# The z-gradient sums go to GpSimd, two on-chip transposes go to the DMA queue, and the bank border of the square products moves: one change to a forward-and-backward kernel of a transformer block

## The chip, the cores and the metric

The kernel runs on one core of a Trainium2 chip. The metric is device time in microseconds of one launch; the runs shown for the kernel before are 823.6, 823.75 and 826.96 us, median 823.75 us. The engines are named as in the profile: PE is the matrix engine (PEld its weight loads), DVE the vector engine, ACT the scalar engine, POOL is GpSimd, and SP is the engine whose queue issues most of the DMAs.

## What is computed

The reference computes a block and its gradients. With S = 2048 rows, D = 640 columns, 32 heads of 20 columns and F = 1728:

```python
# layer A: linear attention, on n = layernorm(x)
q, k, v = split(n @ wqkv)
pq, pk = phi(q), phi(k)                 # phi(t) = t+1 where t>0, else exp(t); plus 1e-6
kv = einsum("bhsd,bhse->bhde", pk, v)   # one 20x20 block per head
z  = einsum("bhsd->bhd", pk)
o  = (pq @ kv) / (pq . z + 1e-6)
h  = x + o @ wo
# layer B: gated MLP, on layernorm(h)
h2 = h + (silu(n2 @ w1) * (n2 @ w3)) @ w2
# results: h2 and the gradients of x, wqkv, wo, w1, w3, w2 for a given grad_out
```

Two intermediate gradients matter here. The gradient of z is a vector of 640 numbers: for each head it is the negative sum over all 2048 rows of r times sn, where r is the query feature divided by its denominator (`r_sb`, 16 tiles of 128 rows) and sn is one number per row and head. The gradient of kv is a 640 x 640 matrix that is not zero only near the 32 diagonal blocks.

## The kernel before

The rows are worked in 16 tiles of 128, the columns in 5 blocks of 128 (DT = 5; `M_H` lists the heads that touch each block). Nothing is reordered by a scheduler: each engine executes its instructions in the order in which the Python code emits them, and waits by semaphores for what others have to deliver. SP's queue is in order too, so an issue that waits holds up every later issue of that queue.

The stages that the change touches, in the order of time:

- **w2 gradient** (loop at line 1018). PE forms 13 products; meanwhile SP loads the transposed weights (`load_w13`, line 988) and the first two blocks of gated gradients (`load_gg`). The last 128 columns of the first weight set are turned on PE: `w13_tail` (line 992) makes 5 transposes, and a DVE copy puts them in place.
- **Stage b** (loop at line 1182, 16 rounds). In round t, PE forms the gradient at the layernorm output for tile t (`b_ghn`, 54 products in 6 parts), and between parts 4 and 5 the product `gr` of tile u = t - 2 (`b_gr`). DVE in each round: `g_h` of tile t - 1 (line 1095), `cc`, `pb` and the reduction `sn` of tile u (lines 1123, 1131, 1132), a negated copy of sn into 32 extra columns behind `g_h` (line 1133), then `wb` twice with two tiny operations between (lines 1085 to 1090), and the two operations of `b_gq` (lines 1138, 1139). POOL has one operation a round, `sz` (line 1135). ACT holds `gs` and `y` of the layernorm backward.
- **wo products** (`q_parts`, line 1143). PE multiplies `r_sb` with `g_h` in 20 parts of 8 products; the first parts stand between the last steps of stage b: part, transposes of `g_h` 14, 2 parts, `gr` 14, transposes of `g_h` 15, 2 parts, `gr` 15, and the rest. In half of them the moving side is 352 columns and not 320: the 32 extra columns carry the negated sn, so that the sums for the z gradient come out of the same products. Line 1160 masks them, line 1253 adds them up.
- **Squares** (`square`, line 1299). A 640 x 640 product with a block-diagonal side: for each of 5 blocks, 6 products, written into two PSUM banks. `SPLIT_D = 19` puts heads 0 to 18 in one bank and 19 to 31 in the other; the border falls inside block 2, so that block is cut into products of 140 and 20 columns. `unload` copies the banks out, one on ACT (380 columns) and one on DVE (260). There are 20 such squares: 5 in an early stage (`f2_wT`, line 686), 5 for `dwoT` (line 1327), 5 for `gm` (line 1352), and 5 in the loop at line 1369.
- **kv gradient**. `gkvT` is formed at line 1318. Its transpose `gkv_b` is made on PE, 13 transposes in the loop at line 1351, each group copied out by DVE. In the same loop the z gradient is spread over a diagonal (line 1360) and brought into all rows by 5 products with a matrix of ones (line 1364).
- **k gradient** (loop at line 1369). For each tile PE forms 10 products into one of 3 `dkv` buffers, DVE adds the z gradient (line 1378) and multiplies by the key features `pkb` (line 1379), which SP loads two tiles at a time (line 1344).

SP issues, around the squares: `xnT` 3, the transposing load of one third of wqkv (`load_wqT(0)`, line 1316), `mN` (line 1337), `dwoT` out (line 1338), four `pkb` loads, five transposes of `gm` (line 1361), `load_wqT(1)` in round 2 of the k loop (line 1393), and four transposing loads `pkT`.

Of the kernel before, what the change touches and what calls it, by code (L numbers as in the profile page):

```python
# [33 lines left out]

M_H = [_heads(m * P, (m + 1) * P, DH) for m in range(DT)]
M_MAX = max(b - a for a, b in M_H)
SPLIT_D = 19


def _pieces(ranges, split, width):  # L40
# [8 lines left out]


SQ = _pieces(M_H, SPLIT_D, DH)
SQ_BLOCKS = [(c, [m for m in range(DT) if M_H[m][0] * DH < (c + 1) * P and M_H[m][1] * DH > c * P]) for c in range(DT)]


@with_exitstack
def kernel(
# [51 lines left out]
    cp = pool("cp")  # L108
    U1 = pool("u1")
# [170 lines left out]
    def two(ap):  # L280
        return ap.rearrange("p (j n) -> p j n", j=2)
# [78 lines left out]
    def heads(ap):  # L360
        return ap.rearrange("p (h e) -> p h e", e=DH)
# [627 lines left out]
        dmaT(out=wT[0][:, 0:FT - 1, :], in_=B_w1[:, 0:F - FL])  # L989
        dmaT(out=wT[1][:], in_=B_w3[:, P - FL:F])  # L990

    def w13_tail():
        tr = ps.tile([P, DT, P], BF16, name="gw", bufs=4)
        for c in range(DT):
            T.transpose(tr[:, c, :], tail[:, c, :], ident[:])
        V.tensor_copy(out=wT[0][:, FT - 1, :].rearrange("p (c q) -> p c q", q=P), in_=tr[:])

    ggb = {}

# [18 lines left out]
    for fc in range(FT - 1):  # L1018
        b, i = divmod(fc, 4)
        if fc == FT - 2:  # L1020
            gw2_tail()
        acc = ps.tile([P, 2, 512], F32, name="gw", bufs=4)
        for j in range(2):
            for t in range(ST):
                T.matmul(acc[:, j, 0:HD], lhsT=hb[b][:, t, i * P:(i + 1) * P], rhs=g2[:, t, j * HD:(j + 1) * HD],  # L1025
                         start=(t == 0), stop=(t == ST - 1))
        ob = br.tile([P, D], BF16, name="gw2o", bufs=2)
        A.copy(out=ob[:].rearrange("p (j n) -> p j n", j=2), in_=acc[:, :, 0:HD])
        A.dma_start(out=out_6[fc * P:(fc + 1) * P, :], in_=ob[:])
# [8 lines left out]
        if fc == FT - 3:  # L1038
            w13_tail()
    ps.release()  # L1040
    U2.release()


    bl = pool("bl")
    g_hx = bl.tile([P, ST, D + H], BF16, name="g_h")
    g_h = g_hx[:, :, 0:D]
    g_q = bl.tile([P, ST, D], BF16, name="g_q")
    bo = pool("bo")
    r_sb = bo.tile([P, ST, D], BF16, name="r_sb")
    ps = pool("pbp", space=PSUM)  # L1050

    gz8 = cp.tile([P, DT, 8], F32, name="gz8")
    V.memset(gz8[:], 0.0)
    gz = cp.tile([P, DT], F32, name="gz")
    hnb, ghT, ln_rest = {}, {}, {}

    def b_load(t):
# [54 lines left out]
        ghT[t] = br.tile([P, DT, P], BF16, name="ghT", bufs=2)  # L1112
        A.copy(out=ghT[t][:], in_=tr[:])

    gr, cc, sz = {}, {}, {}

    def per_head(ap):
        return ap.unsqueeze(2).to_broadcast([P, H, DH])

    def b_gr(t):  # L1120

        cc[t] = br.tile([P, D], F32, name="cc")
        V.tensor_tensor(out=heads(cc[t][:]), in0=heads(r_sb[:, t, :]), in1=per_head(rden[:, t, :]), op=ALU.min)
        gr[t] = ps.tile([P, 2, 512], F32, name="gr", bufs=2)
        for j in range(2):
            for c in range(DT):
                T.matmul(gr[t][:, j, 0:HD], lhsT=ghT[t][:, c, :], rhs=wT2[:, c, j * HD:(j + 1) * HD], start=(c == 0),  # L1127
                         stop=(c == DT - 1))
        pb = br.tile([P, D], F32, name="pb")
        sn = br.tile([P, H], F32, name="sn", bufs=2)  # L1130
        V.tensor_tensor(out=two(pb[:]), in0=gr[t][:, :, 0:HD], in1=two(r_sb[:, t, :]), op=ALU.mult)
        V.reduce_sum(out=sn[:], in_=heads(pb[:]), axis=AX.X)
        V.tensor_scalar(out=g_hx[:, t, D:], in0=sn[:], scalar1=-1.0, scalar2=None, op0=ALU.mult)  # L1133
        sz[t] = br.tile([P, D], F32, name="sz")
        G.tensor_tensor(out=heads(sz[t][:]), in0=heads(Zb[:]), in1=per_head(g_hx[:, t, D:]), op=ALU.mult)  # L1135

    def b_gq(t):
        V.tensor_tensor(out=two(sz[t][:]), in0=gr.pop(t)[:, :, 0:HD], in1=two(sz[t][:]), op=ALU.add)
        V.tensor_tensor(out=g_q[:, t, :], in0=sz.pop(t)[:], in1=cc.pop(t)[:], op=ALU.mult)

    tri = {}

    def q_parts():

        acc = {}
        tags = ("ghn", "ghn", "gr", "ghn", "ghn")
        order = [(0, 0, 0), (0, 0, 1), (1, 0, 0), (1, 0, 1), (0, 8, 0), (1, 8, 0), (2, 0, 0), (2, 0, 1), (0, 8, 1),
                 (1, 8, 1), (2, 8, 0), (2, 8, 1)]
        order += [(m, t0, j) for m in (3, 4) for t0 in (0, 8) for j in range(2)]
        for m, t0, j in order:  # L1150
            if m not in acc:
                acc[m] = ps.tile([P, 2, 512], F32, name="gwo", tag=tags[m], bufs=2)
            n = HD + H * j
            for t in range(t0, t0 + 8):
                T.matmul(acc[m][:, j, 0:n], lhsT=r_sb[:, t, m * P:(m + 1) * P],  # L1155
                         rhs=g_hx[:, t, j * HD:j * HD + n], start=(t == 0), stop=(t == ST - 1))
            if (t0, j) == (8, 1):
                a, b = M_H[m]
                A.copy(out=two(qp[:, m, :]), in_=acc[m][:, :, 0:HD])
                V.tensor_tensor(out=gz8[:, m, 0:b - a], in0=acc.pop(m)[:, 1, HD + a:HD + b], in1=mask[:, m, 0:b - a, 0],  # L1160
                                op=ALU.mult)
                dmaT(out=QT[:, :, m * P:(m + 1) * P], in_=qp[:, m, :])
            yield

# [17 lines left out]
    for t in range(ST):  # L1182
        g = b_ghn(t)

        def part():
            next(g, None)

        u = t - 2
        ahead = 2 <= t <= ST - 4 and t % 2 == 0
        if ahead:  # L1190
            load_gg(t // 2 + 1, 0, FT)
        part()
        part()
        part()
        if t + 2 < ST:
            b_load(t + 2)
        if t >= 1:
            ln_rest.pop(t - 1)()
            if by_dma(t - 1):
                b_gT(t - 1)  # L1200
            if t <= 2 * DT:
                n = (t - 1) % DT
                dst, src = (woT, A_wo) if t <= DT else (kvN, kvT_d)
                A.dma_start_transpose(out=dst[:, :, n * P:(n + 1) * P], in_=src[n * P:(n + 1) * P, :])
            if ahead:
# [12 lines left out]

    tri = U1.tile([P, 2 * DT, D], BF16, name="tri", tag="S0")
    QT, qp = (tri[:, k * DT:(k + 1) * DT, :] for k in range(2))  # L1220
    qg = q_parts()

    def part(n=1):
# [10 lines left out]
    def load_wqT(k):  # L1234
        dmaT(out=wqT[:, k * DT:(k + 1) * DT, :], in_=A_wqkv[:, k * D:(k + 1) * D])
# [100 lines left out]
    gzd = small[:, 3 * DT, :].rearrange("p (m q) -> p m q", q=P)  # L1336
    dma(out=mN, in_=m_v)
    dma(out=rows(dwoT_d), in_=dwoT[:])

# [8 lines left out]
    for n in range(4):  # L1348
        load_pk(n)

    for i, (c, ms) in enumerate(SQ_BLOCKS):
        unload(square(wqT[:, 2 * DT:, :], gkvT, i), gm[:, i, :])
        tr = ps.tile([P, len(ms), P], BF16, name="trk", tag="dkv", bufs=3)
        for k, m in enumerate(ms):
            T.transpose(tr[:, k, :], gkvT[:, m, c * P:(c + 1) * P], ident[:])
        V.tensor_copy(out=gkv_b[:, c, ms[0] * P:(ms[-1] + 1) * P].rearrange("p (i q) -> p i q", q=P), in_=tr[:])
        fill(1)
        if i == 0:
            for m in range(DT):
                V.tensor_scalar(out=gzd[:, m, :], in0=ident[:], scalar1=gz[:, m:m + 1], scalar2=None, op0=ALU.mult)  # L1360
        dmaT(out=wqT[:, 2 * DT:, i * P:(i + 1) * P], in_=gm[:, i, :])
    acc = d_acc()
    for m in range(DT):
        T.matmul(acc[:, m // 4, m % 4 * P:(m % 4 + 1) * P], lhsT=ones[:], rhs=gzd[:, m, :], start=(m % 4 == 0),
                 stop=True, skip_group_check=True)
# [141 lines left out]
```

## Time and profile before

| what | value |
|---|---|
| median of three runs | 823.75 us (823.6 to 826.96) |
| span of the profiled execution | 821.9 us (first to last instruction) |
| median less span | 1.85 us, what lies around the instructions |
| PE busy | 814.4 us |
| PE, from 97 us to the end | busy 720.67 of 725 us |
| DVE, 402 to 538 us (stage b) | busy 90.96 of 136 us |
| POOL, 402 to 538 us | busy 16.65 of 136 us |
| granted clock of TensorE | 1.00 |

The span is that of one profiled execution, so a sum of its rows is compared with 821.9 us, and the 1.85 us are added for a time. "Busy" is the share of time in which an instruction of the engine runs; the chain of waits goes back from the last instruction, at each step to what released it or to the instruction before it.

### The profile page before, as it was taken

To read this page: it belongs to the slowest core of one execution; us is meant where nothing else is said; L and a number is where in the kernel's file an instruction comes from. 1 tells how busy PE (TensorE), PEld (TensorE's weight loads), DVE (VectorE), ACT (ScalarE), POOL (GpSimd) and SP (SyncE) were. 2 spreads that over 40 slices of the span, in tenths; PEclk is the share of its full clock that TensorE was granted. 3 is DMA by queue.
4 is the path that set the end of the run, shared out by engine and by line. 5 is a ranking of instruction groups with operands and counts; after the bars stand their busy time and mean duration, and the time that the engine had idled before them with its cause. 6 is when DMAs were issued, how large, how long until landed. Compare 5 with 4: busy or idle time off the path is not lost.

```text
span 821.9 us, 14179 instructions
## 1 busy us (share of the span) xinstructions
PE 814.4 (99%) x5522; PEld 522.6 (64%) x5549; DVE 453.1 (55%) x961; ACT 325.0 (40%) x609; POOL 133.1 (16%) x194
## 2 busy tenths in 40 slices
PE   8999999999999999999999999999999999999998
PEld 6677544555555555777777777767777777555554
DVE  7869887999898566300057777772681545200000
ACT  7856688665565666011122212222212334211111
POOL 2243333323223212100001111110220000000000
PEclk9999999999999999999999999999999999999999
DMA  9999889696485556999677897258984898885771
GB/s 233 254 279 227 207 234 312 196 242 157 145 213 155 166 181 162 250 241 267 195 170 179 206 204 188 70 113 178 268 216 93 164 200 181 201 199 137 165 170 38
DMA packets 320883, 157.26 MB, mean 191 GB/s; under 512 B 238704, under 2 KB 314064, under 8 KB 320816
## 3 DMA queue, kind: packets, MB, share of 16 engines
q1 hardware_dynamic: 278768, 115.54, 61.3%
q0 software_dynamic: 7328, 24.48, 8.9%
q10 hardware_dynamic: 34720, 16.34, 8.7%
q8 instruction: 43, 0.70, 0.4%
q14 instruction: 24, 0.20, 0.1%
HBM read 47.01 MB, written 51.13 MB: 119 GB/s over the span
## 4 chain that ended last, share of the span: by engine, by line
PE 94%; DVE 2%; ACT 1%; DMA 1%; issue 0%; SPq 0%; POOL 0%; DVEq 0%; ACTq 0%
PE mm L386 20%; PE job L1271 20%; PE ghn L1070 14%; PE gxn L1429 8%; PE o L833 7%; PE gw L1025 7%; PE gwo L1155 3%; PE big L266 3%; PE gr L1127 3%; PE dkv L1375 3%; PE macc L416 2%; PE at L642 2%; DMA wqkv<-in_A_wqkv_dram 1%; PE dkv L1303 1%; DVE st L147 1%; DMA Wp<-pkx 1%
## 5 line engine op out<-in xcount | busy, mean ns | idle before, releaser
L1271 PE MATMUL job<-gb,hnN 128*128 128x432 bf16 (+2 forms) x656 | 117.0, 342 | 0.0
L1070 PEld LDWEIGHTS <-ggb 128*128 128x128 bf16 x864 | 84.5, 98 | 32.8
L1271 PEld LDWEIGHTS <-hnN 128*128 128x128 bf16 x656 | 63.6, 98 | 53.4
L386 PE MATMUL mm<-pqT,w 128*128 128x512 bf16 x397 | 93.1, 379 | 0.5
L386 PEld LDWEIGHTS <-w 128*128 128x128 bf16 x540 | 52.5, 98 | 63.1 <-issue 0.8
L1275 ACT CAST obs<-job 128x432 bf16<-128x432 f32 (+3 forms) x61 | 29.3, 480 | 123.1 <-PE job L1271 123.1
L833 PE MATMUL o<-w,hhT 128*128 128x320 bf16 x448 | 67.7, 299 | 0.1
L1070 PE MATMUL ghn<-w13a,ggb 128*128 128x320 bf16 x448 | 63.5, 299 | 0.0
L1070 PE MATMUL ghn<-w13b,ggb 128*128 128x320 bf16 x416 | 61.4, 299 | 0.0
L386 PE MATMUL mm<-g2T,w2T 128*128 128x512 bf16 x227 | 58.5, 379 | 0.6
L833 PEld LDWEIGHTS <-hhT 128*128 128x128 bf16 x448 | 43.8, 98 | 23.8 <-issue 0.2
L1025 PE MATMUL gw<-g,hb 128*128 128x320 bf16 x416 | 56.8, 299 | 0.0
L1135 POOL TENSOR_TENSOR sz<-Zb,g_h 128x640 f32<-128x640 bf16 x16 | 20.2, 1260 | 198.8 <-DVE g_h L1133 107.7
L1025 PEld LDWEIGHTS <-hb 128*128 128x128 bf16 x416 | 40.6, 98 | 16.0 <-issue 0.3
L1429 PE MATMUL gxn<-wqT,gT 128*128 128x320 bf16 x320 | 48.7, 299 | 0.0
L406 ACT CAST ghh<-mm 128x512 bf16<-128x512 f32 x48 | 28.3, 590 | 44.7 <-PE mm L386 39.0
L772 ACT ACTIVATE sig<-mm 128x512 bf16<-128x512 f32 x56 | 33.9, 605 | 25.1 <-PE mm L386 21.6
L1082 ACT ACTIVATE gs<-ghn 128x640 bf16<-128x640 f32 x16 | 11.2, 703 | 78.9 <-PE ghn L1070 73.4
L386 PEld LDWEIGHTS <-w2T 128*128 128x128 bf16 x260 | 25.4, 98 | 23.3
L266 PEld LDWEIGHTS <-pqT 128*128 128x128 bf16 x320 | 30.6, 98 | 14.4 <-issue 1.7
L1429 PEld LDWEIGHTS <-gT 128*128 128x128 bf16 x320 | 31.3, 98 | 12.2
L266 PE MATMUL big<-wqkv,pqT 128*128 128x320 bf16 x250 | 38.5, 299 | 0.3
(210 smaller groups left out, 1282.3 us busy)
## 6 DMA issues: line engine op xcount, KB each, us to landing
hh_d<-hhT SPq DMA_DIRECT2D x24, 256.0 KB, 2.8
gg_d<-gate POOLq DMA_DIRECT2D x24, 256.0 KB, 4.1
gg_d<-ghh POOLq DMA_DIRECT2D x24, 256.0 KB, 3.5
ggb<-gg_d SPq DMA_DIRECT2D x6, 896.0 KB, 5.4
ggb<-gg_d ACTq DMA_DIRECT2D x6, 832.0 KB, 5.7
out_dram<-obs ACTq DMA_DIRECT2D x39, 108.0 KB, 3.0
x_sb<-in_A_x_dram SPq DMA_DIRECT2D x6, 640.0 KB, 5.4
ggb<-gg_d SPq DMA_DIRECT2D x2, 1728.0 KB, 13.5
```

Source lines behind the costliest of these rows:

```text
L266: T.matmul(acc, lhsT=pqT[:, c, t * P:(t + 1) * P], rhs=wqkv[:, c, n0:n0 + HD], start=(c == 0), stop=(c == DT - 1))
L386: T.matmul(acc[:], lhsT=w[:, c, fc * P:(fc + 1) * P], rhs=rhs[:, c, :], start=(c == 0), stop=(c == DT - 1))
L406: A.copy(out=ghh[n // 2][:, n % 2, :], in_=acc[:])
L772: A.activation(sig[:, i, :], gp[:], AF.Sigmoid)
L833: T.matmul(o2["ps"][:, 0:HD], lhsT=hhT[c][:, fc, i * P:(i + 1) * P], rhs=w2[:, fc, j * HD:(j + 1) * HD], start=(fc == 0), stop=(fc == FT - 1))
L1025: T.matmul(acc[:, j, 0:HD], lhsT=hb[b][:, t, i * P:(i + 1) * P], rhs=g2[:, t, j * HD:(j + 1) * HD], start=(t == 0), stop=(t == ST - 1))
L1070: T.matmul(acc[:, j, 0:HD], lhsT=ggb[t // 2][:, k, lo:lo + P], rhs=rhs[:, j * HD:(j + 1) * HD], start=(k == 0), stop=(k == NG - 1))
L1127: T.matmul(gr[t][:, j, 0:HD], lhsT=ghT[t][:, c, :], rhs=wT2[:, c, j * HD:(j + 1) * HD], start=(c == 0), stop=(c == DT - 1))
L1155: T.matmul(acc[m][:, j, 0:n], lhsT=r_sb[:, t, m * P:(m + 1) * P], rhs=g_hx[:, t, j * HD:j * HD + n], start=(t == 0), stop=(t == ST - 1))
L1271: T.matmul(acc[:, 0:n], lhsT=lhs[:, t, m * P:(m + 1) * P], rhs=rhs(t), start=(t == 0), stop=(t == ST - 1))
L1275: A.copy(out=ob, in_=acc[:, 0:n])
L1429: T.matmul(acc[:, j, 0:HD], lhsT=g, rhs=wqT[:, k, j * HD:(j + 1) * HD], start=(k == 0), stop=(k == 14))
```

## The change

- The 32 extra columns are gone, and with them line 1133, the mask step (line 1160), the sums (line 1253), the diagonal (line 1360). Instead POOL, after its `sz`, multiplies `r_sb` by sn for the tile and subtracts the product from a running sum `gza` (new `b_gz`); at the end DVE splits `gza` into two bfloat16 halves `gzs`, and four products of 320 columns with the ones matrix give the sum over rows.
- `rs`, POOL's product, takes the buffer of `pb`. `sz` is now subtracted and not added.
- The weight tail is turned by one DMA transpose at the end of `load_w13`; the 5 PE transposes and the copy go.
- The 13 PE transposes of `gkvT` and their copies go; five DMA transposes are issued on SP ahead of `mN`.
- `load_wqT(0)` moves from ahead of the kv gradient to round 2 of the k loop, `load_wqT(1)` from round 2 to round 4.
- `SPLIT_D` is 16: block 2 is cut into 80 and 80 columns, the copies are 320 and 320.

```diff
-SPLIT_D = 19
+SPLIT_D = 16
...
         dmaT(out=wT[0][:, 0:FT - 1, :], in_=B_w1[:, 0:F - FL])
         dmaT(out=wT[1][:], in_=B_w3[:, P - FL:F])
-    def w13_tail():
-        tr = ps.tile([P, DT, P], BF16, name="gw", bufs=4)
-        for c in range(DT):
-            T.transpose(tr[:, c, :], tail[:, c, :], ident[:])
-        V.tensor_copy(out=wT[0][:, FT - 1, :].rearrange("p (c q) -> p c q", q=P), in_=tr[:])
+        dmaT(out=wT[0][:, FT - 1, :].rearrange("p (c q) -> p c q", q=P), in_=tail[:].rearrange("p c f -> p (c f)"))
...
-    g_hx = bl.tile([P, ST, D + H], BF16, name="g_h")
-    g_h = g_hx[:, :, 0:D]
+    g_h = bl.tile([P, ST, D], BF16, name="g_h")
...
+    gza = br.tile([P, D], F32, name="gza")
+    G.memset(gza[:], 0.0)
...
         V.reduce_sum(out=sn[:], in_=heads(pb[:]), axis=AX.X)
-        V.tensor_scalar(out=g_hx[:, t, D:], in0=sn[:], scalar1=-1.0, scalar2=None, op0=ALU.mult)
         sz[t] = br.tile([P, D], F32, name="sz")
-        G.tensor_tensor(out=heads(sz[t][:]), in0=heads(Zb[:]), in1=per_head(g_hx[:, t, D:]), op=ALU.mult)
+        G.tensor_tensor(out=heads(sz[t][:]), in0=heads(Zb[:]), in1=per_head(sn[:]), op=ALU.mult)
...
+    def b_gz(t):
+        rs = br.tile([P, D], F32, name="rs", tag="pb")
+        G.tensor_tensor(out=heads(rs[:]), in0=heads(r_sb[:, t, :]), in1=per_head(sns.pop(t)[:]), op=ALU.mult)
+        G.tensor_tensor(out=gza[:], in0=gza[:], in1=rs[:], op=ALU.subtract)
...
-            n = HD + H * j
             for t in range(t0, t0 + 8):
-                T.matmul(acc[m][:, j, 0:n], lhsT=r_sb[:, t, m * P:(m + 1) * P],
-                         rhs=g_hx[:, t, j * HD:j * HD + n], start=(t == 0), stop=(t == ST - 1))
+                T.matmul(acc[m][:, j, 0:HD], lhsT=r_sb[:, t, m * P:(m + 1) * P],
+                         rhs=g_h[:, t, j * HD:(j + 1) * HD], start=(t == 0), stop=(t == ST - 1))
...
         if u >= 0:
             b_gq(u)
+            b_gz(u)
...
-    V.reduce_sum(out=gz[:], in_=gz8[:], axis=AX.X)
+    V.tensor_copy(out=gzs[:, 0, :], in_=gza[:])
+    V.tensor_tensor(out=gzs[:, 1, :], in0=gza[:], in1=gzs[:, 0, :], op=ALU.subtract)
...
     load_xnT(3)
-    load_wqT(0)
     fill(4)
...
+    for m in range(DT):
+        dmaT(out=gkv_b[:, :, m * P:(m + 1) * P], in_=gkvT[:, m, :])
     dma(out=mN, in_=m_v)
...
-        tr = ps.tile([P, len(ms), P], BF16, name="trk", tag="dkv", bufs=3)
-        for k, m in enumerate(ms):
-            T.transpose(tr[:, k, :], gkvT[:, m, c * P:(c + 1) * P], ident[:])
-        V.tensor_copy(out=gkv_b[:, c, ms[0] * P:(ms[-1] + 1) * P].rearrange("p (i q) -> p i q", q=P), in_=tr[:])
         fill(1)
...
-    for m in range(DT):
-        T.matmul(acc[:, m // 4, m % 4 * P:(m % 4 + 1) * P], lhsT=ones[:], rhs=gzd[:, m, :], start=(m % 4 == 0),
-                 stop=True, skip_group_check=True)
-    for x, y, bank in ((0, 4 * P, 0), (4 * P, D, 1)):
-        A.copy(out=gzb[:, x:y], in_=acc[:, bank, 0:y - x])
+    for j in range(2):
+        for k in range(2):
+            T.matmul(acc[:, j, 0:HD], lhsT=ones[:], rhs=gzs[:, k, j * HD:(j + 1) * HD], start=(k == 0), stop=(k == 1))
+    A.copy(out=two(gzb[:]), in_=acc[:, :, 0:HD])
...
-        if t == 2:
-            load_wqT(1)
+        if t in (2, 4):
+            load_wqT(t // 2 - 1)
```

More of the change, by code (lines that the diff above doesn't have):

```diff
@@ L51 @@
 SQ = _pieces(M_H, SPLIT_D, DH)
-SQ_BLOCKS = [(c, [m for m in range(DT) if M_H[m][0] * DH < (c + 1) * P and M_H[m][1] * DH > c * P]) for c in range(DT)]
 @with_exitstack
@@ L1037 @@
             load_gg(1, 0, NG)
-        if fc == FT - 3:
-            w13_tail()
     ps.release()
@@ L1050 @@
     ps = pool("pbp", space=PSUM)
-    gz8 = cp.tile([P, DT, 8], F32, name="gz8")
-    V.memset(gz8[:], 0.0)
-    gz = cp.tile([P, DT], F32, name="gz")
+    gza = br.tile([P, D], F32, name="gza")
+    G.memset(gza[:], 0.0)
     hnb, ghT, ln_rest = {}, {}, {}
@@ L1113, in b_gT @@
         A.copy(out=ghT[t][:], in_=tr[:])
-    gr, cc, sz = {}, {}, {}
+    gr, cc, sz, sns = {}, {}, {}, {}
     def per_head(ap):
@@ L1129, in b_gr @@
         pb = br.tile([P, D], F32, name="pb")
-        sn = br.tile([P, H], F32, name="sn", bufs=2)
+        sn = sns[t] = br.tile([P, H], F32, name="sn", bufs=2)
         V.tensor_tensor(out=two(pb[:]), in0=gr[t][:, :, 0:HD], in1=two(r_sb[:, t, :]), op=ALU.mult)
         V.reduce_sum(out=sn[:], in_=heads(pb[:]), axis=AX.X)
-        V.tensor_scalar(out=g_hx[:, t, D:], in0=sn[:], scalar1=-1.0, scalar2=None, op0=ALU.mult)
         sz[t] = br.tile([P, D], F32, name="sz")
-        G.tensor_tensor(out=heads(sz[t][:]), in0=heads(Zb[:]), in1=per_head(g_hx[:, t, D:]), op=ALU.mult)
+        G.tensor_tensor(out=heads(sz[t][:]), in0=heads(Zb[:]), in1=per_head(sn[:]), op=ALU.mult)
     def b_gq(t):
-        V.tensor_tensor(out=two(sz[t][:]), in0=gr.pop(t)[:, :, 0:HD], in1=two(sz[t][:]), op=ALU.add)
+        V.tensor_tensor(out=two(sz[t][:]), in0=gr.pop(t)[:, :, 0:HD], in1=two(sz[t][:]), op=ALU.subtract)
         V.tensor_tensor(out=g_q[:, t, :], in0=sz.pop(t)[:], in1=cc.pop(t)[:], op=ALU.mult)
+    def b_gz(t):
+        rs = br.tile([P, D], F32, name="rs", tag="pb")
+        G.tensor_tensor(out=heads(rs[:]), in0=heads(r_sb[:, t, :]), in1=per_head(sns.pop(t)[:]), op=ALU.mult)
+        G.tensor_tensor(out=gza[:], in0=gza[:], in1=rs[:], op=ALU.subtract)
     tri = {}
@@ L1152, in q_parts @@
                 acc[m] = ps.tile([P, 2, 512], F32, name="gwo", tag=tags[m], bufs=2)
-            n = HD + H * j
             for t in range(t0, t0 + 8):
-                T.matmul(acc[m][:, j, 0:n], lhsT=r_sb[:, t, m * P:(m + 1) * P],
-                         rhs=g_hx[:, t, j * HD:j * HD + n], start=(t == 0), stop=(t == ST - 1))
+                T.matmul(acc[m][:, j, 0:HD], lhsT=r_sb[:, t, m * P:(m + 1) * P],
+                         rhs=g_h[:, t, j * HD:(j + 1) * HD], start=(t == 0), stop=(t == ST - 1))
             if (t0, j) == (8, 1):
[L1158 to L1161, printed above, removed]
+                A.copy(out=two(qp[:, m, :]), in_=acc.pop(m)[:, :, 0:HD])
                 dmaT(out=QT[:, :, m * P:(m + 1) * P], in_=qp[:, m, :])
@@ L1213 @@
             b_gq(u)
+            b_gz(u)
         if t >= 4:
             load_xn(t - 4, t - 3)
-    tri = U1.tile([P, 2 * DT, D], BF16, name="tri", tag="S0")
-    QT, qp = (tri[:, k * DT:(k + 1) * DT, :] for k in range(2))
+    tri = U1.tile([P, 2 * DT + 2, D], BF16, name="tri", tag="S0")
+    QT, qp, gzs = tri[:, 0:DT, :], tri[:, DT:2 * DT, :], tri[:, 2 * DT:, :]
     qg = q_parts()
@@ L1244 @@
     b_gr(a)
+    b_gz(b)
     part()
     b_gq(a)
+    b_gz(a)
     part(3)
@@ L1335 @@
     mN, gkv_b, gm = (small[:, n:n + DT] for n in (0, DT, 2 * DT))
-    gzd = small[:, 3 * DT, :].rearrange("p (m q) -> p m q", q=P)
+    for m in range(DT):
+        dmaT(out=gkv_b[:, :, m * P:(m + 1) * P], in_=gkvT[:, m, :])
     dma(out=mN, in_=m_v)
@@ L1349 @@
         load_pk(n)
-    for i, (c, ms) in enumerate(SQ_BLOCKS):
+    for i in range(DT):
         unload(square(wqT[:, 2 * DT:, :], gkvT, i), gm[:, i, :])
-        tr = ps.tile([P, len(ms), P], BF16, name="trk", tag="dkv", bufs=3)
-        for k, m in enumerate(ms):
-            T.transpose(tr[:, k, :], gkvT[:, m, c * P:(c + 1) * P], ident[:])
-        V.tensor_copy(out=gkv_b[:, c, ms[0] * P:(ms[-1] + 1) * P].rearrange("p (i q) -> p i q", q=P), in_=tr[:])
         fill(1)
-        if i == 0:
-            for m in range(DT):
-                V.tensor_scalar(out=gzd[:, m, :], in0=ident[:], scalar1=gz[:, m:m + 1], scalar2=None, op0=ALU.mult)
         dmaT(out=wqT[:, 2 * DT:, i * P:(i + 1) * P], in_=gm[:, i, :])
     acc = d_acc()
-    for m in range(DT):
-        T.matmul(acc[:, m // 4, m % 4 * P:(m % 4 + 1) * P], lhsT=ones[:], rhs=gzd[:, m, :], start=(m % 4 == 0),
-                 stop=True, skip_group_check=True)
-    for x, y, bank in ((0, 4 * P, 0), (4 * P, D, 1)):
-        A.copy(out=gzb[:, x:y], in_=acc[:, bank, 0:y - x])
+    for j in range(2):
+        for k in range(2):
+            T.matmul(acc[:, j, 0:HD], lhsT=ones[:], rhs=gzs[:, k, j * HD:(j + 1) * HD], start=(k == 0), stop=(k == 1))
+    A.copy(out=two(gzb[:]), in_=acc[:, :, 0:HD])
     for t in range(ST):
```

## Prediction

> **What bounds the kernel now.** I read the page's busy times first, then the slices, then the chain of waits around the changed stages, then the timelines of DVE, POOL and SP there.
>
> ```profile
> span 821.9 us, 14179 instructions
> ...
> PE 814.4 (99%) x5522; PEld 522.6 (64%) x5549; DVE 453.1 (55%) x961; ACT 325.0 (40%) x609; POOL 133.1 (16%) x194
> ...
> PE   8999999999999999999999999999999999999998
> ...
> POOL 2243333323223212100001111110220000000000
> ```
>
> PE works without a gap: from 97 us to the end it is busy for 720.67 of 725 us, at a granted clock of 1.00, and what is missing there is the wait for the last DMA. Every stage that the change touches but the first squares lies behind 97 us, so a product taken from PE is worth its full spacing, and nothing taken from another engine is worth anything by itself. The reverse is the danger: a wait that the change brings to PE is paid in full, because nothing later can win it back. So there are two sums: what PE loses in work, and what it gains in waits.
>
> **The work taken from PE.** The chain of waits, from 535 to 630 us (start, length, who, how many), has each piece:
>
> ```profile
> 538.09 1.09 PE gwo L1155 x8
> ...
> 539.46 2.28 PE gwo L1155 x16
> ...
> 573.61 0.33 PE dkv L1303 x6
> ...
> 576.88 0.17 PE trk L1355 x3
> ...
> 582.84 0.28 PE dkv L1364 x5
> ```
>
> - Extra columns. Eight products of 320 columns take 1.09 us; the sixteen in the second line are eight of 320 and eight of 352, so eight wide ones take 2.28 - 1.09 = 1.19. There are ten wide groups: 10 x 0.10 = **-1.0 us** (-1.1 if every digit is kept).
> - Transposes of the kv gradient. Five groups, 0.11 + 3 x 0.17 + 0.11 = **-0.73 us**. Weight tail: five transposes, the same kind as in the last line, 0.28: **-0.28 us**.
> - z gradient by ones. Five products of 128 columns (0.28) become four of 320 at 0.136: 0.54, so **+0.26 us**.
> - Squares. The six products take 0.33; the 140-column ones in line 1322 take 1.56/25 = 0.062 each, so 0.02 is left for the 20-column one. From 140 to 320 columns a product grows by 0.074 in 180, so 80 columns take about 0.038, and two of them 0.076 against 0.082. I take -0.01 for a square, 15 squares behind 97 us: **-0.15 us**. Between nothing and -0.3. The five squares ahead of 97 us feed a chain of copies and transposes; ACT's copy gets 60 columns shorter and DVE's 60 longer, and I cost that at nothing, +-0.1.
>
> Together -1.9 us. The DVE operations that go (line 1133 at 0.18, the copies at 0.28 to 0.35, line 1360) are worth nothing: DVE is not on the chain there.
>
> **Wait one: POOL beside DVE in stage b.** A round is 8.69 us (7.33 of `ghn` and 1.36 of `gr` on the chain). One round of DVE and POOL in the timeline:
>
> ```profile
> 449.61 0.82 DVE L1132 TENSOR_REDUCE sn<-pb 128x32 f32<-128x640 f32 x1
> 450.47 0.18 DVE L1133 TENSOR_SCALAR g_h<-sn 128x32 bf16<-128x32 f32 x1
> 450.79 1.26 POOL L1135 TENSOR_TENSOR sz<-Zb,g_h 128x640 f32<-128x640 bf16 x1 [7.43 <-DVE g_h L1133]
> ...
> 452.02 0.83 DVE L1085 SCALAR_TENSOR_TENSOR wb<-gs,hnb 128x640 f32<-128x640 bf16 x1 [1.38 <-ACT gs L1082]
> ...
> 453.09 0.88 DVE L1090 SCALAR_TENSOR_TENSOR wb<-hnb,s,gs 128x640 f32<-128x640 bf16 x1
> ```
>
> `sz` runs while DVE waits for ACT, so the two never meet now. The change puts two more operations of 640 columns behind `sz`. The product `rs` has the shape of `sz`: 1.26. The subtraction reads two float32 operands, which no row shows on POOL; from below 1.26, from above 2.2, if the part of 1.26 that grows with the columns (0.95, from 0.79 at 320 columns to 1.26 at 640) doubled with the bytes. I take 1.26, the row with the same columns. So POOL is busy from 450.6 to 454.5, just where DVE has `wb`, `wb` again, `b_gq` and `g_h`. What meeting costs is seen in an earlier stage:
>
> ```profile
> 67.34 1.53 POOL L358 TENSOR_TENSOR pr<-pql,Zb 128x320 f32<-128x320 bf16 x2 [2.20 <-DVE rden L365]
> 67.69 0.48 DVE L368 TENSOR_SCALAR rden<-rden 128x32 f32<-128x32 f32 x1
> ...
> 68.59 0.97 DVE L372 TENSOR_TENSOR hx<-hx,rden 128x640 bf16<-128x640 bf16 x1
> ```
>
> Line 368 takes 0.18 where POOL is quiet, and line 372, which reads two operands from SBUF, 0.82; here 0.48 and 0.97. POOL's two end at 68.13 and 68.87; 68.17 - 0.18 = 67.99 and 69.56 - 0.82 = 68.74, so both run as if they had started 0.14 us ahead of such an end. The reduction of line 365, with one operand, is no slower under POOL (0.476 against 0.483). So a DVE operation with two SBUF operands waits out a POOL operation. In stage b these are `wb` twice, `g_q`, `g_h` and `cc`: 0.83 + 0.88 + 0.82 + 0.48 + 0.82 = 3.8 us a round, and POOL's three hold 3 x 1.12 = 3.4. That is 7.2 of 8.69, so they fit, but not without waits. Laid out: `wb` wants to start at 452.02, `rs` holds until 453.0; `wb` ends at 453.8 and lets `gza` in, which holds until 454.8; the second `wb` ends at 455.7, 1.7 late. The idle 0.7 ahead of `pb` takes some of it back; carried through the rounds the lag stays at 1.2 to 1.4 and is 1.8 at `g_h` 15. In the middle rounds nobody notices, since `gr` comes two rounds after its `g_h`. At the end PE does: its transposes of `g_h` 15 start at 543.10, and `g_h` 15 is ready at 542.9. Slack about nothing, cost **+1.8 us**. Bounds: 0, if the pieces happen to pass each other, and 15, in the rival below.
>
> [...]
>
> **Wait two: SP ahead of the k gradient.**
>
> ```profile
> 569.65 4.18 SPq L1235 DMA_TRANSPOSE wqT<-in_A_wqkv_dram  x1
> 573.97 0.50 SPq L1337 DMA_DIRECT2D small<-m_d  x1
> 574.94 0.38 SPq L1338 DMA_DIRECT2D dwoT_d<-dwoT  x1
> 575.50 3.88 SPq L1344 DMA_DIRECT2D pkb<-pk_d  x4
> ```
>
> The `mN` issue at 573.97 comes when PE has ended the last `dwoT` square (573.94 on the chain), since its buffer lies over what that square reads. The five new transposes go into the same buffer, so in the changed program the first of them carries this wait, and `mN`, `dwoT` out and `pkb` stand behind all five. The `load_wqT(0)` that is taken away lay ahead of the wait, under cover. Turning 128 x 640 out of SBUF costs SP 1.28 where the queue is quiet (`tri`, two in 2.55) and about 2.0 where it is full (`gm`, five in 9.93). The queue is emptier now, so five at 1.28: 6.4, to 580.4. `mN` then lands after 4.1 (800 KB row: 4.0; 5.9 now, behind the load that goes), 584.5; `dwoT` 2.6 behind it as now, 587.1; the first `pkb` 0.7 later, 587.8. Now it lands at 575.50 + 7.7 = 583.2. DVE wants it at 585.45 less the 0.5 that PE has gained by then. It waits, the three `dkv` buffers fill, and tile 3, due on PE at 588.45 - 0.5 = 587.9, gets its buffer after line 1379 and line 1378 (0.83 each) at 589.5: **+1.6 us**, once, since DVE then has all it needs. Bounds: 0 (lands in time) and 5.6 (transposes at 2.1).
>
> Costed at nothing: the weight tail's DMA shifts the first `ggb` (lands at 394.9, used at 401.7) by 1.3 to 2; the two `load_wqT` come some 10 us later but are first read by `gxn` at 628, and SP is free from 608.9 to 617.9. If that cover failed, `gxn` would start late by what is missing. POOL's sum for tile 15 ends near 560, its copy is needed at 582.
>
> **Sum.** 821.9 - 1.9 + 1.8 + 1.6 = 823.4; with the 1.85 between span and median, **825.2 us**, +0.2%. Half a per cent, 4.1 us, is about what a measurement of this kernel can tell from no change.
>
> **Rivals.**
> 1. *POOL sets the pace of stage b (slower).* DVE's own work is 6.7 us a round. If POOL's operations follow each other before a waiting DVE operation gets in, as at 60.67 us, where line 297 takes 1.86 instead of 0.32 across two of them, a round is 6.7 + 3.4 = 10.1, 1.4 too long, 14 times, less what falls into idle time: +5 to +15, 829 to 838. It decides from 2.0 us of waits a round (8.69 - 6.7). For it: the unknown third operation. Against: line 368 got in between two POOL operations each time, and `gza` waits for `rs`. Chance 0.2.
> 2. *The waits don't come (work only).* -1.9, with one of the two waits at most: 821.8 to 823.5. For it: POOL's turns may fall beside `pb`, `sn` and the `sz` sum, which have one SBUF operand at most. Chance 0.23.
> 3. *SP's transposes at full-queue price.* 825.2 + 4.0 = 829.2. For it: the `gm` rows, and a DMA share of 1.06 from 570 to 580. Chance 0.1.
> 4. My forecast, 823.5 to 828, has 0.47. That the change is not what it says is out: the built order of PE lacks 18 transposes and 80 wide products.
>
> Faster by over half a per cent (below 819.6) would need more than all of the removed work: 0.04. Slower (above 827.9) are rivals 1 and 3 and the edge of my own: 0.33. Within: 0.63. The range 821.2 to 833 leaves out 0.08 below and 0.1 above.
>
> **What would show it.** Line 1085's and 1090's rows of `wb` longer than 0.83 and 0.88, or starting behind POOL's end; a PE gap ahead of the transposes of `g_h` 15 (line 1111) that `g_h` ended; five DMA transposes at 1.3 each from PE's last `dwoT` square, `pkb` landing 12 us after that square, DVE idle ahead of the first `g_k`, and one PE gap of 1 to 2 us in the k loop. If stage b has the same length and no `wb` is late, wait one is wrong; if rounds are longer than 8.69, rival 1 holds.

## The result, and the profile after

The changed kernel takes **836.85 us** (median of five runs, 835.23 to 838.47), the kernel before 823.62 us beside it: ratio 1.0156, 95% interval 1.0142 to 1.017. The forecast was 825.2 us in a range of 821.2 to 833.0: the sign of the shift was right, the size was not, and the time lies outside the range. The profiled execution took 835.23 us, its span is 833.5 us, 11.6 more than before.

The page of the changed kernel, its first line, the line of busy times, and the slices of PE, POOL and the granted clock:

```profile
span 833.5 us, 14169 instructions
...
PE 817.2 (98%) x5503; PEld 522.8 (63%) x5530; DVE 473.2 (57%) x929; ACT 324.7 (39%) x608; POOL 190.6 (23%) x227
...
PE   8999999999999999999999999989799999999998
...
POOL 2243433332223212000035456551120000000000
PEclk9999999999999999999999999999899999999999
```

PE has two dents now, in slices 27 and 29 of 40, and the clock has one digit below full speed. The products are 19 fewer, and yet PE's busy time went up by 2.8 us: some of them ran slower. The waits of PE from 410 to 640 us (who, for whom, us in total, times, longest) name the two dents, and a third wait, at 475 us, that the digits don't show; the kernel before has none there:

```profile
PE dkv L1362 <- DVE gp L1365: 4.5, 1, 4.5
PE ght L1102 <- DVE g_h L1086: 2.1, 1, 2.1
PE gr L1118 <- DMA ghT<-g_h: 2.0, 1, 2.0
```

That is 8.6 us. The rest is in the chain of waits, which has the products behind the waits (start, length, who, how many):

```profile
475.32 2.57 PE gr L1118 x10
477.88 7.98 PE ghn L1061 x54
485.86 1.36 PE gr L1118 x10
487.22 7.33 PE ghn L1061 x54
...
577.08 0.32 PE dkv L1298 x6
...
588.37 7.23 DMA pkb<-pk_d
595.60 0.83 DVE g_k L1366
...
597.40 2.83 PE dkv L1362 x10
600.23 1.99 PE job L1266 x8
602.22 2.72 PE dkv L1362 x20
```

The same ten products of `gr` take 2.57 us behind the first wait and 1.36 one round later; ten of `dkv` take 2.83 behind the last wait and 1.36 (half of 2.72) after that, eight of `job` 1.99 instead of 1.09. The granted clock is 0.55 from 475.3 to 479 us and 0.50 from 597.4 to 601. So two of the three waits were paid twice: 1.21 + 0.65 behind the one at 475, 1.47 + 0.90 behind the one at 597, **4.2 us of slow products**. The line at 577.08 is a square: 0.32 now, 0.33 before.

Cut at the first product of a stage, the 11.6 us are:

| from, to | before | after | difference |
|---|---|---|---|
| start to the first `gw` product | 342.37 | 342.56 | +0.19 |
| to the first `ghn` (holds the weight tail) | 59.19 | 58.91 | -0.28 |
| to the first `gkvT` (stage b, wo products) | 166.83 | 171.86 | +5.03 |
| to the first `gxn` (squares, kv and k gradient) | 59.70 | 65.85 | +6.15 |
| to the end | 193.80 | 194.32 | +0.52 |

Stage b lost 6.0 us by waiting (4.1 idle, 1.9 slow clock) and won 0.96 of work (from the run all_late, below); the k gradient lost 6.9 (4.5 idle, 2.4 slow clock) and won 0.7. My forecast had 1.8 and 1.6 of waits.

Stage b of the changed kernel, one round in the timeline (start, length, engine, line):

```profile
477.97 1.22 ACTq L1098 DMA_TRANSPOSE ghT<-g_h  x1
...
480.34 1.27 POOL L1125 TENSOR_TENSOR sz<-Zb,sn 128x640 f32<-128x640 bf16 x1 [5.08 <-DVE sn L1123]
...
481.57 1.27 POOL L1133 TENSOR_TENSOR rs<-r_sb,sn 128x640 f32<-128x640 bf16 x1
...
482.03 1.49 DVE L1076 SCALAR_TENSOR_TENSOR wb<-gs,hnb 128x640 f32<-128x640 bf16 x1 [1.77 <-ACT gs L1073]
482.92 2.00 POOL L1134 TENSOR_TENSOR gza<-gza,rs 128x640 f32<-128x640 f32 x1
...
483.76 1.84 DVE L1081 SCALAR_TENSOR_TENSOR wb<-hnb,s,gs 128x640 f32<-128x640 bf16 x1
```

The first `wb` waits out `rs`: it ends at 483.52, its 0.82 (the kernel before) would have begun at 482.70, and `rs` ends at 482.84. The second waits out `gza`, 1.84 for the 0.88 of before. This is what the forecast saw in the early stage. Then SP, the same view for the queue's issues:

```profile
578.87 7.68 SPq L1331 DMA_TRANSPOSE small<-bd  x5
586.60 0.57 SPq L1332 DMA_DIRECT2D small<-m_d  x1
...
587.92 3.54 SPq L1339 DMA_DIRECT2D pkb<-pk_d  x4
```

The five transposes start as PE ends the last `dwoT` square (578.80), as forecast, and `pkb` follows 9.05 us later; it stood 1.5 us behind `mN` before. It lands at 595.3, and tile 3 of the k gradient was due on PE at 592.9.

### The profile page after: what moved, and what is told of

The parts are those of the page before. It is cut to its first block, busy times and chain, and to the rows that moved or that the text cites. A ratio compares the mean times of both kernels' runs of the same rounds, so it can differ in the third digit from the quotient of the medians.

```text
span 833.5 us, 14169 instructions
## 1 busy us (share of the span) xinstructions
PE 817.2 (98%) x5503; PEld 522.8 (63%) x5530; DVE 473.2 (57%) x929; ACT 324.7 (39%) x608; POOL 190.6 (23%) x227
## 4 chain that ended last, share of the span: by engine, by line
PE 88%; DMA 5%; DVE 4%; ACT 1%; issue 1%; SPq 1%; ACTq 1%; DVEq 0%
PE mm L385 20%; PE job L1266 19%; PE ghn L1061 9%; PE gxn L1416 8%; PE o L832 7%; PE gw L1020 7%; PE big L265 3%; PE macc L415 2%; PE dkv L1362 2%; PE gwo L1149 2%; PE at L641 2%; PE gr L1118 2%; DVE wb L1081 1%; DMA ghT<-g_h 1%; DVE wb L1076 1%; PE mm L265 1%
## 5 line engine op out<-in xcount | busy, mean ns | idle before, releaser
L1076 DVE SCALAR_TENSOR_TENSOR wb<-gs,hnb 128x640 f32<-128x640 bf16 x16 | 20.8, 1301 | 84.8 <-ACT gs L1073 81.2
L1125 POOL TENSOR_TENSOR sz<-Zb,sn 128x640 f32<-128x640 bf16 x16 | 21.4, 1340 | 151.1 <-issue 89.9
L1266 PEld LDWEIGHTS <-g 128*128 128x128 bf16 x320 | 31.4, 99 | 12.2
```

The costliest lines, as they stand in the source:

```text
L1076: V.scalar_tensor_tensor(out=wb[:], in0=gs[:], scalar=1.0, in1=nrm, op0=ALU.mult, op1=ALU.mult, accum_out=s[:, 1:2])
L1266: T.matmul(acc[:, 0:n], lhsT=lhs[:, t, m * P:(m + 1) * P], rhs=rhs(t), start=(t == 0), stop=(t == ST - 1))
```

## The experiments

Two questions: are there two independent waits, or does one late stage make the other wait; and why is stage b 6 us late, when the holds on DVE are the size that was forecast? All ratios are to the kernel before, with their 95% intervals. "b" is the length from the first `ghn` to the first `gkvT` product (166.83 before), "k" from there to the first `gxn` (59.70), each in the profiled execution.

| kernel | median us | ratio | b | k |
|---|---|---|---|---|
| before | 823.6 to 823.9 | | 166.83 | 59.70 |
| after | 836.85 | 1.0156 [1.0142, 1.017] | 171.86 | 65.85 |
| z_only | 830.61 | 1.0083 [1.0067, 1.01] | 175.29 | 59.96 |
| z_back | 829.12 | 1.0064 [1.005, 1.0077] | 166.83 | 64.33 |
| best | 823.17 | 0.9999 [0.999, 1.0008] | 166.83 | 58.73 |
| after_pkf | 829.88 | 1.0081 [1.0062, 1.0099] | 173.00 | 58.99 |
| z_kvn | 825.2 | 1.0018 [1.0007, 1.003] | 167.19 | 59.96 |
| z_gg | 831.48 | 1.0095 [1.0082, 1.0108] | 174.16 | 59.96 |
| z_rs | 824.9 | 1.0011 [1.0002, 1.002] | 166.56 | 59.97 |
| all_kvn | 824.63 | 1.0005 [0.9995, 1.0015] | 167.21 | 58.99 |
| b_kvn | 823.65 | 0.9994 [0.9982, 1.0006] | 166.83 | 59.70 |
| z_bf | 824.4 | 0.9998 [0.9985, 1.001] | 166.90 | 59.96 |
| all_late | 823.14 | 0.9984 [0.9972, 0.9995] | 165.87 | 59.81 |

### z_only: the z part alone

Against the kernel before:

```diff
-    g_hx = bl.tile([P, ST, D + H], BF16, name="g_h")
+    g_h = bl.tile([P, ST, D], BF16, name="g_h")
...
+            b_gz(u)
...
+            T.matmul(acc[:, j, 0:HD], lhsT=ones[:], rhs=gzs[:, k, j * HD:(j + 1) * HD], start=(k == 0), stop=(k == 1))
```

> The kernel before with the z part alone: GpSimd sums the z gradient, no extra product columns; the kv gradient, the weight tail and the squares stay as they were. Theory A (two independent waits: GpSimd holds up VectorE in stage b, and SP's five transposes hold up the loads of the k gradient): this kernel has only the first. From the profile of after: 4.1 us of PE idle in stage b (1.97 and 2.14), about 1.4 us of lower clock behind the first of them, less 1.0 - 0.26 of removed products: about +5, 827.5 to 830. Rival B (one cause: the late end of stage b shifts everything behind it, and the wait at the k gradient comes from that): nearly all of the +13 is here, 833 to 837. My forecast on record would have had 824.7 here.

830.61 us (828.71 to 832.93): theory A's size, 0.6 above its range (the profiled execution is the longest of the four, 832.93, so its b is perhaps 2 us above that of the median; only one execution has a profile). Stage k is +0.26 as forecast, so the late stage b doesn't make the second wait. In stage b PE waits four times, three times for `ghT` (1.87, 1.42, 2.75) and once for `g_h` 15 (1.15).

### z_back: the z part undone

Against the changed kernel:

```diff
-    g_h = bl.tile([P, ST, D], BF16, name="g_h")
+    g_hx = bl.tile([P, ST, D + H], BF16, name="g_h")
...
-            b_gz(u)
```

> The changed kernel with the z part undone (product columns as before, no sum on GpSimd); kv gradient and weight tail by DMA and the new bank border stay. Theory A: only the second wait, 4.5 us of PE idle ahead of the third tile of the k gradient and about 2.4 us of lower clock behind it, less 1.16 of removed work (0.73 + 0.28 + 0.15): about +5.7, 828 to 830.5, and stage b as in before (rounds of 8.69 us, wb at 0.83 and 0.88). Rival B: the wait shrinks to nothing without the late stage b, 822 to 824.5. My forecast on record would have had 824.1 here.

829.12 us, as theory A has it. Stage b has exactly the length of before. The two parts make +6.95 and +5.46 against the 823.66 of the kernel before beside them, 12.4 together, and the whole change has 13.2: two waits, nearly independent. Rival B falls. Here the second wait can be read without the first: PE stands idle for 3.88 us until 591.75, and the ten `dkv` products behind it take 2.83.

### best and after_pkf: pkb ahead of the transposes on SP

One edit, in best against z_back and in after_pkf against the changed kernel:

```diff
-    for m in range(DT):
-        dmaT(out=gkv_b[:, :, m * P:(m + 1) * P], in_=gkvT[:, m, :])
-    dma(out=mN, in_=m_v)
-    dma(out=rows(dwoT_d), in_=dwoT[:])
...
     for n in range(4):
         load_pk(n)
+    dma(out=mN, in_=m_v)
+    for m in range(DT):
+        dmaT(out=gkv_b[:, :, m * P:(m + 1) * P], in_=gkvT[:, m, :])
+    dma(out=rows(dwoT_d), in_=dwoT[:])
```

> As z_back, but the four pkb loads and the mN load are issued on SP ahead of the five transposes of the kv gradient, and the dwoT store behind them. Theory A (the order on SP's queue is the cause): the wait is gone, only the removed work is left: -1.16, 822.1 to 823.2, no PE idle in the k loop, clock 1.00 there. Rival C (the DMA rings are full at that point and pkb lands some 7 us after its issue and too late in any order, or the transposes slow what lands beside them): the idle in the k loop stays at 2 us or more, 826 or more.

> The whole changed kernel with the same new order on SP (pkb and mN loads ahead of the five transposes). Theory A: stage b's wait remains, the second is gone: z_only less about 1.2, 826.5 to 829. Rival B: the wait is moved, not removed: 833 or more. The two theories also differ on the sum: by A, (z_only - before) + (z_back - before) is after - before = 13.2 within 1.5; by B the sum is far smaller or larger.

SP in the first of the two, issues in the timeline:

```profile
570.49 1.94 SPq L1334 DMA_DIRECT2D pkb<-pk_d  x4
574.32 0.37 SPq L1340 DMA_DIRECT2D small<-m_d  x1
574.78 8.30 SPq L1342 DMA_TRANSPOSE small<-bd  x5
```

`pkb` is issued before PE ends the last square, lands at 573.7, and PE has no gap in the k loop: stage k is 0.97 shorter than before. The transposes take even longer than in the changed kernel (8.30 against 7.68), and nobody waits for them. So it is the order on SP, and rival C falls. As a time the gain is too small to be told from no change: 0.9999. In the whole change the same order takes 7 us off (836.85 to 829.88, 0.9 above the expected range, as z_only's own time was higher) and leaves z_only's wait.

### z_kvn: the wo and kv transposes behind gs, and b_kvn, its control

Where the lag of stage b comes from is seen on ACT in z_only, one round in its timeline:

```profile
478.67 1.22 ACTq L1105 DMA_TRANSPOSE ghT<-g_h  x1
479.93 1.30 ACTq L1202 DMA_TRANSPOSE kvN<-kvT_d  x1
481.26 0.59 ACTq L1003 DMA_DIRECT2D ggb<-gg_d  x1
481.90 0.70 ACT L1080 ACTIVATE gs<-ghn 128x640 bf16<-128x640 f32 x1 [4.24 <-DMA ghT<-g_h]
...
488.33 1.31 ACTq L1105 DMA_TRANSPOSE ghT<-g_h  x1
```

ACT takes these in order. `g_h` of the last round releases its `ghT` issue, behind that stand `kvN` and `ggb`, and only then `gs`, which feeds DVE's `wb` and, 6.43 us later, the next `g_h`. From `ghT` to `ghT` it is 9.66 here, 8.65 to 9.66 in the eight rounds from 432 to 508 us, 9.4 on average, and a round of PE is 8.69. In all of these rounds `gs` starts 0.05 us behind the end of the last issue, so ACT's queue sets its time. In the kernel before the step from `gs` to `ghT` is 4.80 (468.58 to 473.38). The issues take 2.6 in one round and 3.6 to 4.5 in the next, so the loop is 7.4 and 8.4 to 9.3 by turns, 8.1 on average: a long round is won back in the next, where `gs` has 0.4 to 1.3 us to spare. The added 1.6 of DVE holds would fit into the two rounds of slack once; in the loop they come again in each round. The edit of z_kvn, against z_only (b_kvn has the same against the kernel before):

```diff
-            if t <= 2 * DT:
-                n = (t - 1) % DT
-                ...
-                A.dma_start_transpose(out=dst[:, :, n * P:(n + 1) * P], in_=src[n * P:(n + 1) * P, :])
             if ahead:
                 load_gg(t // 2 + 1, FT, NG, A.dma_start)
...
             b_gq(u)
             b_gz(u)
+        if 1 <= t <= 2 * DT:
+            ...
+            A.dma_start_transpose(out=dst[:, :, n * P:(n + 1) * P], in_=src[n * P:(n + 1) * P, :])
```

> z_only (the kernel before with the z gradient summed by GpSimd, 830.6), and the ten transposes of wo and kv that ACT issues in stage b moved in ACT's order from behind the ghT transpose to behind the round's gs. Theory L (a loop between DVE and ACT): g_h lets ACT issue ghT (1.22), woT or kvN (1.30) and at times ggb (0.6), and only then comes gs, which DVE's wb waits for; in z_only gs to ghT takes 6.43 where before has 4.79, so the loop is 9.2 to 9.7 and longer than PE's round of 8.69, and the lag grows by up to 1 us a round for as long as these transposes are there. Without the 1.30 the loop is 7.7 to 8.3 and fits: no PE idle in the middle of stage b, only some 1 to 1.5 us at the last g_h: 823.5 to 826. Rival P (GpSimd's holds alone make DVE's round too long): the loop changes nothing, 829 to 832.

> The control for z_kvn: the kernel before with only the ten wo and kv transposes moved behind gs on ACT. In before the loop of DVE and ACT (4.79 from gs to ghT, 2.6 to 3.3 of issues) is shorter than PE's round of 8.69, so by theory L the move is worth nothing here: 823 to 825, stage b as long as in before. If the move is worth something by itself (822 or less), z_kvn's gain over z_only is partly that.

825.2 us: 5.4 of the 7.0 are gone, and the control shows that the move is worth nothing by itself (0.9994). The holds are all still there, in the groups of DVE in stage b (line, operation, busy us, mean ns):

```profile
L1088 DVE SCALAR_TENSOR_TENSOR wb<-hnb,s,gs 128x640 f32<-128x640 bf16 x16 | 24.1, 1505 | 0.0
L1136 DVE TENSOR_TENSOR g_q<-sz,cc 128x640 bf16<-128x640 f32 x16 | 19.8, 1238 | 0.6
L1083 DVE SCALAR_TENSOR_TENSOR wb<-gs,hnb 128x640 f32<-128x640 bf16 x16 | 19.1, 1196 | 30.6 <-ACT gs L1080 30.6
```

The second `wb` has 1505 ns for 882, `g_q` 1238 for 825, the first `wb` 1196 for 825; from `gs` to `ghT` it is 6.41, as in z_only. But `ghT` follows `ghT` after 8.65, `gs` starts 0.2 us or more behind the issues, and PE waits once, 1.28 us for `g_h` 15. So the loop through ACT, not the holds alone, made the loss: theory L holds, rival P falls.

### z_gg: the big load behind ghT

In z_only PE's waits in the middle come where SP's load of `ggb` (896 KB) is issued beside a `ghT` transpose:

```profile
488.33 1.31 ACTq L1105 DMA_TRANSPOSE ghT<-g_h  x1
...
488.62 0.38 SPq L1003 DMA_DIRECT2D ggb<-gg_d  x1
...
494.90 1.53 PE L1125 MATMUL gr<-wT,ghT 128*128 128x320 bf16 x10 [1.42 <-DMA ghT<-g_h]
```

The transpose lands at 494.86 and the load at 494.81, 6.5 us behind the issue of the transpose; in the changed kernel nine of the 14 `ghT` land 2.6 to 2.9 us behind theirs. In the kernel before, `ghT` is issued 3.0 to 3.9 us ahead of each of the six loads of SP and lands 2.6 to 2.7 us behind its issue, before the load is issued. Why the two land together was not shown by a run. The edit, against z_only:

```diff
         if ahead:
-            load_gg(t // 2 + 1, 0, FT)
+            pass
...
             if ahead:
+                load_gg(t // 2 + 1, 0, FT, A.dma_start)
                 load_gg(t // 2 + 1, FT, NG, A.dma_start)
```

> z_only with the first half of each ggb load issued by ACT behind that round's ghT and kvN transposes, ahead of the second half, and not by SP at the start of the round. In z_only each of the three PE gaps in the middle of stage b (1.87, 1.42, 2.75) comes with a ghT transpose that was issued within 0.3 us of SP's ggb load and landed together with it, 6.5 to 7.5 us later, where 2.7 is usual. Theory L with these collisions as its end: the three gaps go, but the loop gets longer by the issue (0.4 to 0.6 in every second round), so the lag reaches PE some rounds later as waits for ghT without a collision, and in the end for g_h 15: 828 to 833. Rival C (the collisions alone are the loss): 824 to 826, with the gap at the end alone.

831.48 us. The collisions are gone, two waits for `ghT` of 0.66 and 0.85 and one for `ggb` of 0.49 are left of them, and the lag arrives at the end: PE waits 3.76 us for `g_h` 15, with a slow clock behind. Rival C falls: a collision decides where the lag is paid, not whether.

### z_rs, z_bf: less work on GpSimd

Against z_only, first z_rs, which leaves the sum out, then z_bf, which leaves the product with sn out:

```diff
-        G.tensor_tensor(out=gza[:], in0=gza[:], in1=rs[:], op=ALU.subtract)
...
-        G.tensor_tensor(out=heads(rs[:]), in0=heads(r_sb[:, t, :]), in1=per_head(sns.pop(t)[:]), op=ALU.mult)
-        G.tensor_tensor(out=gza[:], in0=gza[:], in1=rs[:], op=ALU.subtract)
+        G.tensor_tensor(out=gza[:], in0=gza[:], in1=r_sb[:, t, :], op=ALU.subtract)
```

> z_only without the subtraction that adds up gza: the products rs are made, the sum over the tiles is left out, so the z gradient is that of a zero sum. GpSimd has 1.26 + 1.27 a round instead of 1.26 + 1.27 + 2.00. Theory L: the second wb is not held any more (0.88), the first still is (1.49), gs to ghT falls from 6.43 to about 5.5, the loop to 8.0 to 8.7, and it fits: 823.5 to 826. Rival P' (each operation that is added costs its share): about half of the +7 stays, 827 to 828.5.

> z_only with GpSimd's second and third operation replaced by one: gza minus the bfloat16 tile of r itself (the product with sn is left out, so the z gradient is wrong in value). It tells what makes the subtraction 2.00 long. If it is the second float32 operand: 1.27, as sz and rs have with a bfloat16 operand; if it is that the result goes back to where the first operand is, or the two separate tensors: about 2.0. By theory L the time follows: with 1.27 as z_rs (824 to 826), with 2.0 somewhat more (825 to 828), since the first wb is then held longer.

824.9 and 824.4 us: with one added operation instead of two the loop fits, and PE waits only for `g_h` 15 (0.66 and 1.00). That is not half of the +7, as a price per operation would have it, but nearly all. The question of the type has an answer that neither side expected: the subtraction with a bfloat16 operand takes 1.39 us at least, 1.40 in the median of its 16 and 2.07 at most; the one with two float32 operands takes 1.54 in the changed kernel the one time that nothing runs on DVE beside it (at 562.80), and 1.99 to 2.02 the 15 other times, beside a `wb` or a `g_q`. So 0.46 of the 2.00 goes with what runs on DVE.

### all_kvn, all_late: the whole change, mended

The first is the changed kernel with the edits of after_pkf and z_kvn; the second has further (and six buffers for sn instead of two, which the late sums need):

```diff
-            b_gz(u)
+            if u < 12:
+                b_gz(u)
...
-    b_gz(b)
     part()
     b_gq(a)
-    b_gz(a)
+    for u in range(12, ST):
+        b_gz(u)
```

> The whole changed kernel with both repairs: pkb and mN loads ahead of the five transposes on SP (after_pkf, 829.9), and the wo and kv transposes behind gs on ACT. Theory L: the removed work (-1.9) and about +1 to +1.5 of wait for the last g_h are left: 822.5 to 824.5, no difference to before that can be measured. Rival P: 828 or more.

> all_kvn with GpSimd's sums for the last four tiles put behind the last g_q of stage b, where VectorE is idle. In all_kvn PE waits 1.30 for g_h of tile 15, because DVE's operations of the rounds before are held by the sums. Theory L: with no sum in the last rounds that gap goes, and only the removed work is left: 821.5 to 823.2 (before 823.9), no PE idle between 97 us and the end. If the gap stays above 0.8, the lag comes from sz alone or from earlier rounds, and the time is that of all_kvn, 824.6.

824.63 us, 0.1 above its range and not to be told from before; with the last four sums moved 823.14 us, ratio 0.9984 [0.9972, 0.9995]. In its profile PE is busy for all of 430 to 550 us and no wait for `g_h` is left. There is one of 0.64 at 569.86, where `gkvT` waits for the transposes of `QT`: the wo products now end 0.96 earlier, so a DMA is late next. Its median is 0.16% below the kernel before, with an interval that just leaves out 1, and 1.6% below the changed kernel. Of the 1.95 us of work that is gone its median shows 0.8; the profile has this wait of 0.64 and one of 0.44 for `gT`, behind the first `gxn`. What GpSimd's moved sums cost is seen in its timeline:

```profile
554.20 2.00 POOL L1134 TENSOR_TENSOR gza<-gza,rs 128x640 f32<-128x640 f32 x1
...
557.62 1.54 POOL L1134 TENSOR_TENSOR gza<-gza,rs 128x640 f32<-128x640 f32 x1
```

The first stands beside a `g_q` on DVE (553.78 to 554.80), the second beside nothing.

## Why the prediction was wrong, step by step

- **The work: right.** -1.9 was forecast. Measured by stage: -0.28 (weight tail, forecast -0.28), -0.96 (extra columns, all_late; -1.0), -0.97 (kv transposes and squares, best; -0.88), +0.26 (ones product, z_only; +0.26): -1.95.
- **Wait one: the holds right, the step behind them wrong.** "Carried through the rounds the lag stays at 1.2 to 1.4", with "in the middle rounds nobody notices", is the step that failed. The lag of one round is 1.6 (6.41 against 4.80, z_kvn), and where the loop is opened the wait at `g_h` 15 is 1.28, near the forecast 1.8. What I left out is what a late `g_h` releases on ACT: `ghT`, `kvN`, `ggb`, and behind them the `gs` of the next round. I had asked who waits behind the late DVE operation on PE, and not on ACT. 1.8 was forecast, 6.0 measured. `gza` was taken at 1.26 and had 2.00, inside the bounds. One row behind the holds was misread: line 368 (`rden<-rden`) reads one tensor and was held too (0.48 for 0.18), so it doesn't show that two SBUF operands are the condition, and no run does. What the runs show is which operations were held: `wb`, `wb` and `g_q` in z_kvn (1.20, 1.50 and 1.24 on average, for 0.83, 0.88 and 0.83 before), and not `sz<-gr,sz`, which took 0.81 to 0.83 the nine times that it ran beside `rs` or `gza` in the changed kernel.
- **Rival 1 had the size, but not the reason.** It gave 829 to 838 for the case that DVE's waits exceed 2.0 a round. In z_kvn the held operations are 0.37, 0.62 and 0.41 longer on average, 1.4 a round, and its time is 825.2.
- **Wait two: the mechanism right, the size not.** Without the first wait (z_back) the five transposes took 6.78 (forecast 6.4), `mN` landed 5.6 behind its issue (4.1), `dwoT` and `pkb` in steps of 2.5 and 0.65 (2.6 and 0.7); so `pkb` came 1.9 later than forecast, DVE began 0.3 after it landed, and PE's tile, due at 587.87 as forecast (587.9), waited 3.88 and not 1.6. The 4.1 rested on a row of 4.0 of the same size, a store near 714 us (`out_dram<-g_h`); without `load_wqT(0)` ahead of it `mN` went from 5.9 only to 5.6. In the changed kernel the transposes took 7.68, and the wait was 4.49.
- **The term that was not in the sum: the clock.** Each wait was costed by its length. Two of the three in the changed kernel were followed by products at about half the clock, 4.2 us in all, a third of the loss; the section on the hardware shows which waits those are. With it z_back's wait costs 3.88 + 1.73 = 5.6, just my upper bound, and the changed kernel's 6.9, beyond it.
- **Rival 3** (transposes of 2.1 each) is not it: 6.78 to 7.68 for five. **Costed at nothing:** the `ggb` and `load_wqT` moves were cheap; behind the first `gxn` the change has +0.5, of which one wait for `gT` (0.21) is seen. The same wait, 0.17 to 0.46, stands in z_back, after_pkf, all_kvn and all_late, and not in best, z_only or before; its cause was not followed.

## What to carry to other kernels

When an operation gets later, follow what it releases on every engine that works in order, DMA issues among them, until you come back to where you started: if the loop is longer than a round, a fixed delay is paid in each round and slack of two rounds doesn't help. Put the load that the next step waits for ahead of new issues on its queue, above all ahead of issues that wait. And cost a wait of the matrix engine of about two microseconds or more with the slow products that may come behind it, 1.7 to 2.4 us here.

## What the runs showed of the hardware

**The clock after a wait of PE.** The granted clock in the windows behind each wait:

| wait of PE, us | kernel | granted clock behind it |
|---|---|---|
| 0.49 to 1.88 (14 waits) | z_only, z_gg, after_pkf, z_kvn, all_kvn, z_rs, z_bf, all_late | 1.00 |
| 1.97 | after | 0.55 over 3.7 us |
| 2.05 | after_pkf | 1.00 |
| 2.14 | after | 1.00 |
| 2.75 | z_only | 0.81, then 0.50 over 2 us, then 0.82 over 2 us |
| 3.76 | z_gg | 0.69, then 0.50 over 2 us, then 0.90 |
| 3.88 | z_back | 0.50 over 3.3 us |
| 4.49 | after | 0.50 over 3.6 us |

So near 2 us the length alone doesn't decide. The clock record of the changed kernel has the half clock from 475.64 to 479.06 us and from 595.11 to 601.94, for 3.41 and 6.83 us; in z_only and z_gg an estimate from the shares of the windows is 516.3 to 519.7 and 550.0 to 553.4. In the 3.41 us ahead of these four starts PE was idle for 1.97, 2.19, 2.3 and 2.9 us. The wait of 2.14 in the changed kernel is longer than the first of them, and the clock stayed at 1.00. What differs in that trace is where they lie: its four changes of the clock are 3.41, 116.05 and 6.83 us apart, 1, 34 and 2 times 3.41, and in steps counted so the wait of 2.14 lies across a border at 547.32, 0.60 and 1.54 of it in one step each, where the wait of 1.97 lies in one step and the wait of 4.49 has 2.19 and 2.29 in two; no other step has more idle time than the 1.54. No run moved a wait on purpose, so this is read off one trace and not tested, and the wait of 2.05 in after_pkf stays open. The loss by slow products is 1.7 to 2.4 us for a wait (1.73 in z_back, 1.86 and 2.37 in the changed kernel).

**GpSimd waited too.** In the changed kernel `gza` took 1.99 to 2.02 us the 15 times that a `wb` or a `g_q` ran beside it on DVE and 1.54 the one time that nothing did; `rs` took 1.85 where a `wb` was running as it began (at 435.29) and 1.27 where none was (at 481.57). With the `wb` of 1.49 and 1.84 beside them the holds went both ways.

**A small transpose landed with the big load of another queue.** A `ghT` landed 2.6 to 2.9 us behind its issue nine of 14 times in the changed kernel, and 6.9 us behind it where the load was issued 0.17 us later (at 468.32 and 468.49); in z_only it took 6.5 to 7.5 the three times that the two were issued within 0.3 us of each other. Issued 1.1 us ahead of the load, it took 2.7 and 2.9 (changed kernel, at 505.94 and 450.01).
